# Token groups laid out in fours in the routing of a fused attention, feed-forward and mixture-of-experts kernel

## The chip, the cores and the metric

The kernel runs on one core of a Trainium2 chip. The metric is device time in microseconds (us), from the start to the end of one execution. Several executions were timed, and one more was recorded by the profiler.

A core has a matrix engine (TensorE; PE in the profile, PEld for its weight loads), three engines for elementwise work (VectorE is DVE, ScalarE is ACT, GpSimd is POOL), and queues that start DMA transfers (SP above all). Each engine works through its own list of instructions in order and waits on semaphores for the others.

## The reference, cut to what matters

```python
x = attn(r, k, v, w, u)                  # 4 x 768 tokens, 8 heads of 48: 3072 x 384
h = np.maximum(x @ w_in, 0.0)            # d_ff 2048
x = (h * h) @ w_out
logits = x @ w_gate                      # 3072 x 8
for idx in np.argsort(-logits.flatten()):        # greedy, best pair first
    tok, e = int(idx) // 8, int(idx) % 8
    if assigned[tok] >= 0 or counts[e] >= 384:   # an expert takes 384 tokens
        continue
    assigned[tok] = e; counts[e] += 1
for e in range(8):
    out[assigned == e] = np.maximum(x[assigned == e] @ w1[e], 0.0) @ w2[e]
```

The order of the greedy assignment is what the routing part of the kernel reproduces. Each expert ends with exactly 384 tokens.

## The kernel before, in words

Everything is in float32, and products are formed with each operand split in a high and a low part, so that one product is three matmuls. The program has three stages. Up to about 150 us, the attention is begun together with the preparation of the feed-forward weights. Up to about 591 us, eight blocks of 384 tokens go through the feed-forward layer (`mm1`, line 414, and `mm2`, line 458), with the rest of the attention woven in; in the first part of that a guard (lines 209 to 218) reads the weights once more and takes a minimum on VectorE. From about 601 us, the eight experts are computed one after another (`up`, line 828, and `down`, line 842).

The experts are filled one by one, in the order in which they run full ("phases"). For one phase the 3072 tokens lie as 128 partitions by 24 groups (NG = 24). Each token has its best remaining logit, scaled to a number `yb`. The kernel finds the threshold above which some expert has 384 tokens, in three rounds of a search with 128 steps (NS = 3):

- `above` (line 701) writes, on VectorE, an indicator for each token and each of 128 thresholds: one if `yb` is at least the threshold. It lies in two tiles `I` of 128 thresholds by 12 groups in bfloat16 (GH = 12), made by one instruction each (line 705). The thresholds come from the table `num` (line 531), where each number 0 to 127 stands 24 times; of each 24 the instruction reads the first 12.
- `count` (line 709) sums over tokens on TensorE: 24 weight loads of 128 thresholds, one for each group, each followed by a matmul with the 8 one-hot columns of that group (line 712). For one group the 128 thresholds lie 12 elements, 24 bytes, apart.
- `reached` (line 717) sums a flag over partitions (line 719, the weights are the constant `ones`, which lie side by side), and `narrowed` (line 724) sets the next `yb` and calls `above` again.

After three rounds `choose` (736) and `place` (752) fix the expert and each token's slot. `indices_d` (line 625) writes a one-hot `oi` of the slot for each token, 128 by 24 groups in bfloat16, one VectorE instruction of 3072 elements (line 632). `tokens` (line 639) takes `oi` as weights of 24 matmuls with 6 columns (line 642); there, the 128 weights of one group lie 24 elements, 48 bytes, apart. `gather` (line 650) then fetches the token rows by indirect DMA, and `turn` (line 657) transposes them for the expert.

There are 21 counts (7 phases of 3; the last phase takes what is left) and 8 `tokens`. All of this is put, by lists of numbered slots (FIRST, NEXT, PLAN1, PLAN2, PLAN), between the matmuls of the feed-forward layer's last block and of the experts that run meanwhile. These stages are recorded in the order in which they are written. The stage with the guard, from about 137 to 560 us, is ordered by a scheduler that uses its own estimate of each instruction's duration. The scaled values for the first phase are made there in two pieces: 21 groups early, and 3 groups once the last block's logits are there. The scratch tiles `sm` hold all small tensors of a phase, one behind the other, in words of 4 bytes (class `Small`, line 603); on them the address of `yb` and `ib` depends.

Of the kernel before, what the change touches and what calls it, by code (L numbers as in the profile page):

```python
# [9 lines left out]
BF = mybir.dt.bfloat16  # L10
# [3 lines left out]
OP = mybir.AluOpType  # L14
# [7 lines left out]
def kernel(ctx, tc, r, k, v, w, u, w_in, w_out, w_gate, w1, w2, out):  # L22
    nc = tc.nc
# [11 lines left out]
    E = w_gate.shape[1]  # L35
# [4 lines left out]
    NG = NB * CB  # L40
    NJ = 64
    NT = 128
    GH = NG // 2
# [3 lines left out]
    CT = CAP // 128  # L47
    consts = ctx.enter_context(tc.tile_pool(name="consts", bufs=1))
# [6 lines left out]
                            base=0, channel_multiplier=1)  # L55
# [6 lines left out]
    wk = ctx.enter_context(tc.tile_pool(name="wk", bufs=2))  # L62
# [10 lines left out]
    def piece(shape, dtype, name):  # L73
        return wk.tile(shape, dtype, name=name, tag="w", bufs=NW)
# [45 lines left out]
    g, gk = gt[:, 0], gt[:, 1]  # L120
# [399 lines left out]
    def some():  # L520
        nonlocal pos, todo
        todo += per
        while todo >= 1 and pos < len(segs):
            for x in segs[pos]:
# [3 lines left out]

    LAG = 2

    num = consts.tile([128, 128, NG], BF, name="num")
    nc.gpsimd.iota(num, pattern=[[1, 128], [0, NG]], base=0, channel_multiplier=0,
                   allow_small_or_imprecise_dtypes=True)
    code = consts.tile([128, E], FT, name="code")
    nc.gpsimd.iota(code, pattern=[[-1, E]], base=E, channel_multiplier=0, allow_small_or_imprecise_dtypes=True)
# [11 lines left out]
                            channel_multiplier=-1)  # L547
# [74 lines left out]
    def rp(name="pr"):  # L622
        return abank([128, 512], name)

    def indices_d(st, si):
        sm = st["sm"]
        nc.vector.tensor_scalar(si[:, 1], si[:, 0], 127, None, op0=OP.bitwise_and)
        nc.vector.tensor_scalar(si[:, 2], si[:, 0], 7, None, op0=OP.arith_shift_right)
        ib = sm([128, NG], BF)
        nc.vector.tensor_copy(ib, si[:, 1])  # L630
        st["oi"] = oi = piece([128, 128, NG], BF, "oi")
        nc.vector.tensor_tensor(oi, ib[:, None, :].to_broadcast([128, 128, NG]), num, op=OP.is_equal)
        oq = sm([128, NG, CT], FT)
        nc.vector.tensor_tensor(oq, si[:, 2, :, None].to_broadcast([128, NG, CT]), q3, op=OP.is_equal)
        st["ov"] = ov = sm([128, NG, 2, CT], BF)
        nc.vector.tensor_scalar(ov[:, :, 0], oq, pc, None, op0=OP.mult)
        nc.vector.tensor_tensor(ov[:, :, 1], oq, gg, op=OP.mult)

    def tokens(ph, st):
        p = rp()  # L640
        for g in range(NG):
            nc.tensor.matmul(p[:, :2 * CT], st["oi"][:, :, g], st["ov"][:, g].rearrange("p a b -> p (a b)"),  # L642
                             start=(g == 0), stop=(g == NG - 1))
        f = st["sm"]([128, CT], FT)
        nc.vector.tensor_copy(f, p[:, CT:2 * CT])
        idx = idxs[:, E if ph == "again" else ph]
        nc.vector.scalar_tensor_tensor(idx, f, 128.0, p[:, :CT], op0=OP.mult, op1=OP.add)
        IDX[ph] = idx
# [19 lines left out]
    def route(ph):  # L668
        st = {}

        def best(g0=0, g1=NG):
            n = g1 - g0
            if not g0:
                st["sm"] = sm = Small(2)
                st["v"] = sm([128, NG], FT)
                st["c"] = sm([128, NG, E], FT)
                st["oh"] = sm([128, NG, E], BF)
                st["cc"] = sm([128, NG], FT)
                for nm, shape, dt in (("y", [128, NG], FT), ("yb", [128, NG], BF), ("fl", [128, E], BF),
                                      ("mx", [128, 1], FT)):  # L680
                    st[nm, 0], st[nm, 1] = sm(shape, dt), sm(shape, dt)
                st["y"], st["yb"] = st["y", 0], st["yb", 0]
                halves()
            v, c, oh, cc, y, yb = (st[x][:, g0:g1] for x in ("v", "c", "oh", "cc", "y", "yb"))
            l = lg[:, g0:g1]
            vb = v[:, :, None].to_broadcast([128, n, E])
            nc.vector.tensor_reduce(v, l, axis=X, op=OP.max)
            nc.vector.tensor_scalar(yb, v, rng[:, 3:4], rng[:, 2:3], op0=OP.subtract, op1=OP.mult)
            nc.vector.tensor_tensor(oh, l, vb, op=OP.is_equal)
            above(g0, g1)  # L690
            nc.vector.tensor_tensor(c, l, vb, op=OP.is_equal)
            nc.vector.tensor_tensor(c, c, code[:, None, :].to_broadcast([128, n, E]), op=OP.mult)
            nc.vector.tensor_reduce(cc, c, axis=X, op=OP.max)
            nc.vector.tensor_scalar(y, v, rng[:, 3:4], rng[:, 2:3], op0=OP.subtract, op1=OP.mult)
            nc.vector.tensor_scalar(y, y, 1.0 + SLACK, None, op0=OP.add)


        def halves():
            st["I"] = [wk.tile([128, NT, GH], BF, name="I", tag="dd", bufs=2) for _ in range(2)]

        def above(g0=0, g1=NG):
            for i, t in enumerate(st["I"]):
                a, b = max(g0, i * GH), min(g1, (i + 1) * GH)
                if a < b:
                    nc.vector.tensor_tensor(t[:, :, a - i * GH:b - i * GH],  # L705
                                            st["yb"][:, None, a:b].to_broadcast([128, NT, b - a]),
                                            num[:, :, :b - a], op=OP.is_ge)

        def count(k):
            p = rp()  # L710
            for g in range(NG):
                nc.tensor.matmul(p[:, :E], st["I"][g // GH][:, :, g % GH], st["oh"][:, g], start=(g == 0),  # L712
                                 stop=(g == NG - 1))
            st["fl"] = fl = st["fl", k % 2]
            nc.vector.tensor_scalar(fl, p[:, :E], float(CAP), None, op0=OP.is_ge)
# [8 lines left out]
        def narrowed(k):  # L724
            _, mx = reached(k)
            y = st["y", (k + 1) % 2]
            st["yb"] = yb = st["yb", (k + 1) % 2]
            nc.vector.tensor_scalar(yb, st["y"], mx, float(RAD), op0=OP.subtract, op1=OP.mult)  # L728
            halves()
            above()  # L730
            if k < NS - 2:
                nc.vector.tensor_scalar(y, st["y"], mx, float(RAD), op0=OP.subtract, op1=OP.mult)
                nc.vector.tensor_scalar(y, y, 1.0 + SLACK, None, op0=OP.add)
                st["y"] = y
# [53 lines left out]
        for k in range(0 if steps else NS):  # L788
            steps.append(lambda k=k: count(k))
            steps.append((lambda k=k: narrowed(k)) if k < NS - 1 else lambda: (choose(), fetch(ph)))  # L790
        steps += [place, lambda: indices_d(st, st["si"]), lambda: tokens(ph, st), lambda: gather(ph, st)]
        return best, steps + [lambda q=q: turn(ph, st, q) for q in range(CT)]

# [65 lines left out]
    for g in range(NF, NB * NF):  # L859
        m, f = divmod(g, NF)  # L860
# [37 lines left out]
    for n in range(NF * CB):  # L898
        f, t = divmod(n, CB)
        if f >= NF - LF:  # L900
            t, f = divmod(n - (NF - LF) * CB, LF)
# [8 lines left out]
    for c in range(1, E):  # L910
        s0 = NFE * (c - 2)
        p, first = PLAN1 if c == 1 else PLAN2 if c == 2 else PLAN
# [112 lines left out]
    def exact(ph):  # L1025
# [76 lines left out]
        nc.vector.tensor_copy(si[:, 0], sl)  # L1102
        st = {"sm": sm}
        indices_d(st, si)
        tokens(ph, st)
        gather(ph, st)
        m = sm([128, NG, E], I32)
# [95 lines left out]
```

## Time and profile before

| What | Value |
|---|---|
| runs | 873.54, 874.99, 875.88 us (median 874.99) |
| the profiled execution's own time | 871.84 us |
| its span, first to last instruction | 869.3 us |
| busy share | PE 95%, PEld 90%, DVE 62%, ACT 40%, POOL 16% |
| mean granted TensorE clock | 0.982 of full speed |
| chain that ended last | PE 77%, DMA 6%, DVE 6%, issue 5%, SPq 3%, ACT 2%, POOL 1% |

The chain is followed back from the last instruction to what released each step, so its shares say where the time was spent that could not be hidden. A busy share is an average over stages that differ: VectorE is at 62% over the whole, but at over 80% in the stage of the experts' routing. The profiled execution ran 2.5 us outside its span.

### The profile page before, as it was taken

The numbers are of one execution on the slowest core, as the hardware profiler recorded it, in microseconds if no ns is written. First come the engines' busy times: TensorE is split into PE (matmuls) and PEld (weight loads), VectorE is DVE, ScalarE is ACT, GpSimd is POOL, SyncE is SP. The second block draws the span as 40 slices with busy tenths as digits, with TensorE's granted clock in tenths as the row PEclk, the third lists the DMA queues.
The fourth block names the chain that finished last, engine by engine and source line by source line (L and its number), as shares of the span: only waits on it lengthen the run. The fifth ranks groups of instructions, "written<-read, shape, count | busy, mean of one in ns | idle before, by whom it ended". The sixth has DMA issues, their size and how long they took to land.

```text
span 869.3 us, 15596 instructions
## 1 busy us (share of the span) xinstructions
PE 822.3 (95%) x6069; PEld 779.2 (90%) x6069; DVE 540.5 (62%) x1172; ACT 349.1 (40%) x761; POOL 136.3 (16%) x188
## 2 busy tenths in 40 slices
PE   5669999999999999999999999997989999999996
PEld 4569988899999999999999999896989999999996
DVE  6969879864445444444435435646977888885551
ACT  4467554335325334435335324302333443334441
POOL 5402103111111111111111000001102113113311
PEclk9989999999999999999999999997999999999999
DMA  9998357842122122122121000013334355345430
GB/s 178 186 222 201 84 143 216 238 104 56 28 41 55 29 41 55 29 42 55 28 38 33 1 15 27 1 43 121 115 97 128 119 155 161 104 137 164 146 119 31
DMA packets 120211, 82.32 MB, mean 95 GB/s; under 512 B 80321, under 2 KB 111681, under 8 KB 120129
## 3 DMA queue, kind: packets, MB, share of 16 engines
q1 hardware_dynamic: 114608, 69.14, 31.8%
q0 software_dynamic: 3072, 9.44, 3.4%
q10 hardware_dynamic: 2448, 2.66, 1.5%
q8 instruction: 50, 0.82, 0.4%
q14 instruction: 33, 0.26, 0.1%
HBM read 69.42 MB, written 9.44 MB: 91 GB/s over the span
## 4 chain that ended last, share of the span: by engine, by line
PE 77%; DMA 6%; DVE 6%; issue 5%; SPq 3%; ACT 2%; POOL 1%; POOLq 0%; DVEq 0%
PE acc L458 21%; PE p L414 21%; PE q L828 10%; PE ad L842 9%; PE pr L712 3%; DMA raw<-in_moe_w_in_dram 3%; PE pa L331 2%; PE py L345 2%; PE py L351 2%; PE pr L642 2%; DMA gd<-in_moe_w_out_dram 1%; DVE lg L218 1%; SPq L87 1%; PE pu L384 1%; PE lt L475 1%
## 5 line engine op out<-in xcount | busy, mean ns | idle before, releaser
L414 PE MATMUL p<-xT,wi 128*128 128x384 f32 x1152 | 227.2, 342 | 10.6 <-DMA xT<-xT 7.0
L414 PEld LDWEIGHTS p<-xT,wi 128*128 128x128 f32 x1152 | 205.0, 190 | 14.2 <-issue 7.4
L458 PE MATMUL acc<-wo,h 128*128 128x392 f32 x1008 | 204.2, 347 | 0.0
L458 PEld LDWEIGHTS acc<-wo,h 128*128 128x128 f32 x1008 | 177.4, 188 | 4.9 <-issue 2.6
L425 DVE TENSOR_TENSOR s<-a,p 128x384 f32<-128x384 f32 x112 | 61.8, 553 | 144.7 <-ACT a L420 144.6
L420 ACT ACTIVATE a<-p 128x384 f32<-128x384 f32 x128 | 62.3, 488 | 164.9 <-PE p L414 131.8
L842 PE MATMUL ad<-we,he 128*128 128x384 f32 x576 | 117.8, 345 | 0.0
L828 PE MATMUL q<-xe,we 128*128 128x384 f32 x576 | 114.8, 343 | 0.8 <-ACT xe L665 0.6
L828 PEld LDWEIGHTS q<-xe,we 128*128 128x128 f32 x576 | 102.4, 191 | 1.8 <-ACT xe L665 0.8
L842 PEld LDWEIGHTS ad<-we,he 128*128 128x128 f32 x576 | 100.8, 191 | 0.4 <-issue 0.4
L831 ACT ACTIVATE he<-q 128x384 fp32r<-128x384 f32 x64 | 31.5, 493 | 143.7 <-PE q L828 123.0
L432 ACT ACTIVATE h<-s 128x384 fp32r<-128x384 f32 x112 | 58.8, 526 | 70.5 <-DVE s L425 64.1
L437 DVE TENSOR_TENSOR h<-s,h 128x384 fp32r<-128x384 f32 x112 | 63.3, 567 | 20.1 <-ACT h L432 19.7
L295 ACT ACTIVATE dd<-ident,c 128x128 f32<-128x128 f32 x192 | 59.1, 392 | 18.2 <-DVE c L289 10.5
L832 DVE SCALAR_TENSOR_TENSOR he<-q,he 128x384 fp32r<-128x384 f32 x64 | 35.6, 556 | 46.9 <-ACT he L831 46.6
L83 POOL MEMSET rkv<- 128x384 f32 x24 | 9.8, 418 | 261.4 <-PE py L345 261.4
L849 POOL DMA_INDIRECT out_dram<-oe,idxs x24 | 27.7, 1155 | 140.2 <-ACT oe L847 136.8
L336 DVE COPY_PREDICATED dd<-msk,pa 128x512 f32<-128x512 int32 x48 | 33.9, 734 | 21.1 <-PE pa L331 21.1
L654 POOL DMA_INDIRECT xg<-x,idxs x24 | 25.9, 1080 | 103.5 <-DVE sm L728 33.0
L705 DVE TENSOR_TENSOR I<-sm,num 128x1536 bf16<-128x1536 bf16 (+2 forms) x43 | 39.1, 948 | 0.5
L712 PEld LDWEIGHTS <-I 128*128 128x128 bf16 x504 | 31.9, 159 | 6.2 <-DVE I L705 3.0
L283 POOL TENSOR_TENSOR tmp<-rkv 128x384 f32<-128x384 f32 x24 | 27.3, 1139 | 54.4 <-ACT s L423 31.8
(192 smaller groups left out, 987.3 us busy)
## 6 DMA issues: line engine op xcount, KB each, us to landing
w1r<-in_moe_w_dram SPq DMA_DIRECT2D x32, 384.0 KB, 3.1
w2r<-in_moe_w_dram SPq DMA_DIRECT2D x32, 384.0 KB, 3.8
raw<-in_moe_w_out_dram SPq DMA_DIRECT2D x8, 768.0 KB, 5.4
gd<-in_moe_w_in_dram SPq DMA_DIRECT2D x16, 384.0 KB, 3.6
gd<-in_moe_w_out_dram SPq DMA_DIRECT2D x16, 384.0 KB, 3.9
rkv<-in_k_dram SPq DMA_DIRECT2D x24, 192.0 KB, 3.2
rkv<-in_r_dram SPq DMA_DIRECT2D x24, 192.0 KB, 4.1
rkv<-in_v_dram SPq DMA_DIRECT2D x24, 192.0 KB, 4.7
```

The costliest lines, as they stand in the source:

```text
L295: nc.scalar.activation(d[:, h], ident, AF.Copy, scale=c[:, h:h + 1])
L414: nc.tensor.matmul(p, WI[f // PO][:, wl, d, fs], x[:, hl, d], start=(n == 0), stop=(n == 3 * KD - 1))
L420: nc.scalar.activation(a, p, AF.Relu)
L425: nc.vector.tensor_tensor(s, a, p, op=OP.mult)
L432: nc.scalar.activation(h[:, 0], s, AF.Copy)
L437: (eng or nc.vector).tensor_tensor(h[:, 1], SM.pop(f), h[:, 0].bitcast(FT), op=OP.subtract)
L458: nc.tensor.matmul(acc[t][:, c0:], h[:, hl, t * 128:(t + 1) * 128], WO[f // PO][:, wl, f % PO, c0:], start=(f == 0 and n == 0), stop=(f == ...
L705: nc.vector.tensor_tensor(t[:, :, a - i * GH:b - i * GH], st["yb"][:, None, a:b].to_broadcast([128, NT, b - a]), num[:, :, :b - a], op=OP. ...
L712: nc.tensor.matmul(p[:, :E], st["I"][g // GH][:, :, g % GH], st["oh"][:, g], start=(g == 0), stop=(g == NG - 1))
L828: nc.tensor.matmul(p, wt[:, wl, d, fs], x[:, hl, d], start=(n == 0), stop=(n == 3 * KD - 1))
L832: nc.vector.scalar_tensor_tensor(h[:, 1], p, 0.0, h[:, 0].bitcast(FT), op0=OP.max, op1=OP.subtract)
L842: nc.tensor.matmul(ac2[t], h[:, hl, t * 128:(t + 1) * 128], wt[:, wl, f % P2], start=(f == 0 and n == 0), stop=(f == NFE - 1 and n == 2))
```

## The change

The table `num` holds each number 4 times instead of 24. The indicators are laid out as (3 fours of groups) x 128 thresholds x 4 groups in each of the two tiles, and the one-hots as 6 x 128 x 4. For one group, the 128 weights of a load now lie 4 elements, 8 bytes, apart. One instruction still makes a whole tile: it runs over fours of groups, within these over the 128 numbers, within these over 4 groups. Where a piece doesn't begin or end on a four, `above` issues an instruction more.

```diff
-    num = consts.tile([128, 128, NG], BF, name="num")
-    nc.gpsimd.iota(num, pattern=[[1, 128], [0, NG]], base=0, channel_multiplier=0,
+    NP_ = 4
+    num = consts.tile([128, 128, NP_], BF, name="num")
+    nc.gpsimd.iota(num, pattern=[[1, 128], [0, NP_]], base=0, channel_multiplier=0,
...
-        st["oi"] = oi = piece([128, 128, NG], BF, "oi")
-        nc.vector.tensor_tensor(oi, ib[:, None, :].to_broadcast([128, 128, NG]), num, op=OP.is_equal)
+        st["oi"] = oi = piece([128, NG // NP_, 128, NP_], BF, "oi")
+        nc.vector.tensor_tensor(oi, ib.rearrange("p (a o b) -> p a o b", o=1, b=NP_).to_broadcast([128, NG // NP_, 128, NP_]),
+                                num[:, None].to_broadcast([128, NG // NP_, 128, NP_]), op=OP.is_equal)
...
-            nc.tensor.matmul(p[:, :2 * CT], st["oi"][:, :, g], st["ov"][:, g].rearrange("p a b -> p (a b)"),
+            nc.tensor.matmul(p[:, :2 * CT], st["oi"][:, g // NP_, :, g % NP_], st["ov"][:, g].rearrange("p a b -> p (a b)"),
...
-            st["I"] = [wk.tile([128, NT, GH], BF, name="I", tag="dd", bufs=2) for _ in range(2)]
+            st["I"] = [wk.tile([128, GH // NP_, NT, NP_], BF, name="I", tag="dd", bufs=2) for _ in range(2)]
...
-                if a < b:
-                    nc.vector.tensor_tensor(t[:, :, a - i * GH:b - i * GH],
-                                            st["yb"][:, None, a:b].to_broadcast([128, NT, b - a]),
-                                            num[:, :, :b - a], op=OP.is_ge)
+                while a < b:
+                    o = a % NP_
+                    n = NP_ if not o and b - a >= NP_ else min(NP_ - o, b - a)
+                    m = (b - a) // NP_ if n == NP_ else 1
+                    x = (a - i * GH) // NP_
+                    nc.vector.tensor_tensor(
+                        t[:, x:x + m, :, o:o + n],
+                        st["yb"][:, a:a + m * n].rearrange("p (a o b) -> p a o b", o=1, b=n).to_broadcast([128, m, NT, n]),
+                        num[:, None, :, :n].to_broadcast([128, m, NT, n]), op=OP.is_ge)
+                    a += m * n
...
-                nc.tensor.matmul(p[:, :E], st["I"][g // GH][:, :, g % GH], st["oh"][:, g], start=(g == 0),
+                nc.tensor.matmul(p[:, :E], st["I"][g // GH][:, g % GH // NP_, :, g % NP_], st["oh"][:, g], start=(g == 0),
```

TensorE, ScalarE and the SP queue have the same instructions in the same order as before. VectorE and GpSimd differ at three places. The first is VectorE where the first phase's indicators for 21 groups are made (`keep` and `s` belong to the feed-forward layer's last block, `rng` to the scaling). Before:

```order
L437 TENSOR_TENSOR keep<-s,keep 128x384
L705 TENSOR_TENSOR I<-sm,num 128x1536
L425 TENSOR_TENSOR s<-a,p_5709 128x384
L705 TENSOR_TENSOR I<-sm,num 128x128x9
L437 TENSOR_TENSOR keep<-s,keep 128x384
```

And of the changed kernel:

```order
L437 TENSOR_TENSOR keep<-s,keep 128x384
L711 TENSOR_TENSOR I<-sm,num 128x1536
L425 TENSOR_TENSOR s<-a,p_5709 128x384
L711 TENSOR_TENSOR I<-sm,num 128x1024
L711 TENSOR_TENSOR I<-sm,num 128x128
L437 TENSOR_TENSOR keep<-s,keep 128x384
```

The second tile's 9 groups are made by two instructions, 8 groups and 1 group. The second place is VectorE at about 144 us, in the guard (`gd` is a piece of weights, `lg` here its running minimum, `c`, `rkv` and `dd` belong to attention unit 6, `s` and `h` to the feed-forward layer). Before:

```order
L425 TENSOR_TENSOR s<-a,p_1574 128x384
L218 SCALAR_TENSOR_TENSOR lg_66<-gd,lg_66 128x192
L277 TENSOR_TENSOR rkv<-rkv,tk 128x8x48
L437 TENSOR_TENSOR h_1588<-s,h_1588 128x384
L289 TENSOR_REDUCE c<-tmp 128x8
L218 SCALAR_TENSOR_TENSOR lg_66<-gd,lg_66 128x192
L336 COPY_PREDICATED dd<-msk,pa 128x4x128 x2
L425 TENSOR_TENSOR s<-a,p_1623 128x384
```

And of the changed kernel:

```order
L425 TENSOR_TENSOR s<-a,p_1574 128x384
L277 TENSOR_TENSOR rkv<-rkv,tk 128x8x48
L289 TENSOR_REDUCE c<-tmp 128x8
L437 TENSOR_TENSOR h_1588<-s,h_1588 128x384
L218 SCALAR_TENSOR_TENSOR lg_66<-gd,lg_66 128x192 x2
L336 COPY_PREDICATED dd<-msk,pa 128x4x128
L425 TENSOR_TENSOR s<-a,p_1623 128x384
L336 COPY_PREDICATED dd<-msk,pa 128x4x128
```

The scheduler counts the shorter table as done earlier, and lets two attention steps go ahead of pieces of the guard; some ten rows later the two orders agree again. The third place is GpSimd just before, where the tables are made: one memset (`rkv`, line 83) now stands behind three short instructions for `tri`, `ones` and `onef` instead of ahead of them.

## Rows read from the trace of the kernel before

**Rows 1.** The page's chain that ended last, by line.

```profile
PE acc L458 21%; PE p L414 21%; PE q L828 10%; PE ad L842 9%; PE pr L712 3%; DMA raw<-in_moe_w_in_dram 3%; PE pa L331 2%; PE py L345 2%; PE py L351 2%; PE pr L642 2%; DMA gd<-in_moe_w_out_dram 1%; DVE lg L218 1%; SPq L87 1%; PE pu L384 1%; 
```

**Rows 2.** Windows: stretch, its us, then busy us by engine, clock, DMA.

```profile
600.00:633.00 33.00, 30.14 (x219) 27.46 (x220) 27.23 (x68) 11.84 (x20) 4.10 (x6) 0.86 0.45 131
633.00:666.00 33.00, 30.14 (x213) 28.78 (x212) 24.90 (x69) 10.79 (x20) 8.01 (x9) 0.95 0.33 103
...
732.00:765.00 33.00, 33.00 (x256) 31.80 (x255) 27.49 (x68) 12.58 (x24) 7.14 (x9) 1.00 0.43 133
```

**Rows 3.** Chain of waits in order of time, 720 to 746 us: start, us, what.

```profile
722.88 1.65 PE pr L642 x24
...
733.12 1.45 PE pr L712 x24
...
740.53 1.41 PE pr L712 x24
```

**Rows 4.** Groups by line and shape: count | busy us, mean ns | idle before.

```profile
L705 DVE TENSOR_TENSOR I<-sm,num 128x1536 bf16<-128x1536 bf16 x41 | 37.5, 954 | 0.5
...
L632 DVE TENSOR_TENSOR oi<-sm,num 128x3072 bf16<-128x3072 bf16 x8 | 14.1, 1759 | 0.3
...
L705 DVE TENSOR_TENSOR I<-sm,num 128x1152 bf16<-128x1152 bf16 x1 | 0.9, 902 | 0.0
...
L705 DVE TENSOR_TENSOR I<-sm,num 128x384 bf16<-128x384 bf16 x1 | 0.7, 743 | 0.0
```

**Rows 5.** The same view, weight loads whose weights lie strided, and side by side.

```profile
L712 PEld LDWEIGHTS <-I 128*128 128x128 bf16 x504 | 31.9, 159 | 6.2 <-DVE I L705 3.0 <-issue 2.1 <-DVE sm L695 0.5
...
L642 PEld LDWEIGHTS <-oi 128*128 128x128 bf16 x192 | 13.9, 176 | 1.3 <-issue 1.3
...
L719 PEld LDWEIGHTS <-ones 128*128 128x128 bf16 x21 | 2.1, 101 | 2.1 <-issue 1.8
```

**Rows 6.** Timeline, 745.2 to 745.5 us: two pairs with weights side by side.

```profile
745.16 0.10 PEld L755 LDWEIGHTS <-ones 128*128 128x128 bf16 x1 [0.16 <-issue]
745.17 0.19 PE L755 MATMUL pr<-sm,ones 128*128 128x24 bf16 x1
745.18 0.10 PEld L756 LDWEIGHTS <-tri 128*128 128x128 bf16 x1
745.21 0.17 PE L756 MATMUL pr<-sm,tri 128*128 128x24 bf16 x1
```

**Rows 7.** Waits of PE, 545 to 860 us: total us, times, longest.

```profile
PE pr L593 <- DVE m L591: 2.9, 1, 2.9
PE px L663 <- DMA xg<-x,idxs: 2.3, 3, 1.4
PE pr L712 <- DVE I L705: 1.8, 2, 1.5
```

**Rows 8.** Chain of waits, 590 to 606 us, before the first expert.

```profile
596.93 3.98 DMA xg<-x,idxs
...
600.96 0.92 PE px L663 x3
```

**Rows 9.** Timeline of all engines, 738.6 to 741.9 us: a third round's indicators and count.

```profile
738.70 1.83 DVE L705 TENSOR_TENSOR I<-sm,num 128x1536 bf16<-128x1536 bf16 x2
...
740.37 1.57 PE L712 MATMUL pr<-sm,I 128*128 128x8 bf16 x24
```

**Rows 10.** Timeline of all engines, 624 to 627 us: the second expert's indices and gather.

```profile
625.50 0.15 DVE L645 COPY sm<-pr 128x3 f32<-128x3 f32 x1
...
626.64 0.95 POOL L654 DMA_INDIRECT xg<-x,idxs  x1 [25.30 <-DVE idxs L647]
```

**Rows 11.** Chain of waits, 150 to 172 us, in the guard.

```profile
161.38 4.45 DMA gd<-in_moe_w_out_dram
...
168.57 3.10 PE p L414 x9
```

**Rows 12.** Groups by line: the table's instruction on POOL.

```profile
L532 POOL IOTA num<- 128x3072 bf16 x1 | 3.3, 3341 | 0.0
```

## The prediction

> **What bounds the kernel now.** I read the chain that ended last first. Nearly all of its weight lies on TensorE: the feed-forward layer and the experts, and behind them 3% on line 712 (the counts) and 2% on line 642 (the token sums) [rows 1]. Then the windows. In the routing of the middle phases TensorE is busy for 33.0 of 33 us at the full clock, with VectorE at 27.5; in the first 66 us of the experts TensorE leaves 2.9 us in each 33 and VectorE works 27.2 and 24.9 [rows 2]. So a TensorE instruction saved there comes off the end, as long as VectorE, which has some 5.5 us to spare per phase of 33 us, delivers in time. The chain in order of time gives the price of the two loops that the change touches: 24 pairs of weight load and matmul take 1.41 to 1.45 us in a count and 1.65 us in the token sum [rows 3], that is 60 and 69 ns for one pair. The columns that stream through (8 and 6) can't explain that; the fewer take longer. What differs is how far apart the weights lie: one load takes 159 ns at 24 bytes, 176 ns at 48 bytes, and 101 ns where they lie side by side, 2 bytes apart [rows 5].
>
> **TensorE: 29 loops with weights 8 bytes apart.** No row shows 8 bytes. From one side, it is no better than 24 bytes: 60 ns, and the counts win nothing (the token sums 9 ns a pair). From the other, it is like side by side. The two pairs with such weights that follow each other start their matmuls 40 ns apart (745.17 and 745.21) and their loads 20 ns apart [rows 6]; that is a pair alone, and a stream of 24 might run below 40. A straight line from 40 ns at 2 bytes to 60 at 24 gives 45 at 8. The value lies 6 bytes from the one row and 16 from the other, so I keep near the first and take 42 ns; the ends that I keep are 30 (halfway between the starts of loads and of matmuls) and 60. At 42 a count gets shorter by 24 x 18 ns = 0.43 us and a token sum by 24 x 27 ns = 0.65 us. The 504 loads of line 712 are 21 counts, the 192 of line 642 are 8 token sums [rows 5]. Where they lie decides what arrives:
> - Three counts and one token sum stand between the last matmuls of the feed-forward layer. They end that layer earlier, and with it the stores that the first gather waits for: 3 x 0.43 + 0.65 = 1.94 us.
> - Two counts fall into the wait for that gather (it is 3.98 us, and the first transpose comes at 600.96) [rows 8]: 0.
> - One count at 609 us: 0.43.
> - One token sum and two counts lie at 621 to 632 us, 1.51 us. The second expert's gather starts at 626.64, behind indices that come at 625.50 [rows 10] out of VectorE's queue, which is full there [rows 2], and transposes have waited for gathers already (2.3 us in three waits) [rows 7]. TensorE would only wait longer; I count 0.2.
> - One count at 636 us: 0.43. The wait for line 591 behind it (2.9 us) [rows 7] starts from TensorE's own result, and moves along.
> - One token sum and three counts at 656 to 676 us; the last one's result waits in VectorE's queue, so 0.65 + 2 x 0.43 + 0.2 = 1.71.
> - Five token sums and nine counts from 689 us on, where TensorE has no gap: 5 x 0.65 + 9 x 0.43 = 7.12.
>
> Together 1.94 + 0.43 + 0.2 + 0.43 + 1.71 + 7.12 = 11.8 us. With 30 ns in place of 42 it is 18.5, with 60 ns only the 9 ns of the token sums are left, 7 x 0.22 = 1.5.
>
> The Trainium skill has a rule for this spacing (Advanced Engine Details and Errata, SBUF Cachelines): the memory is read in lines of 16 bytes, and a reader keeps its full speed if it takes at least two elements of each line. At 8 bytes there are two weights to a line, at 24 and 48 one; by it a pair would cost the 40 ns of the side-by-side row, and the sum would be 13.0 us in place of 11.8. The trace agrees as far as it goes (101 ns against 159 and 176).
>
> **VectorE: the same elements in shorter runs.** The whole tiles keep their 1536 and 3072 elements. The rows at 954 and 1759 ns give 0.524 ns for an element and 149 ns fixed [rows 4], so two elements a cycle are being made now, with runs of 12 and 24. For runs of 4 I take no extra cost. The bounds: nothing is gained, since the elements stay. Against me stands the form with runs of 9, which should take 753 ns by that slope and takes 902 [rows 4]: 149 ns for 128 runs, 1.16 ns each. With 384 runs of 4 that would be 0.45 us on each indicator and, with 768, 0.89 us on each one-hot. The end of the scale is that the pairing is lost: 0.80 and 1.61 us. I stay at 0, because the 9 is odd and leaves half a pair in every run, as 4 and 12 do not. If the cover goes, the third count of a phase suffers first. Its second indicator ends at 740.53, 0.16 us after the count has begun at 740.37 [rows 9]; it is needed by the count's second half only, 0.72 us in now and 0.50 us in at 42 ns. So 0.3 us remain.
>
> One page speaks against the one-hots alone: the Trainium skill (Vector Engine (DVE) Microarchitecture Reference, Measured stream behaviour on trn2) has full rate for runs of two words of 4 bytes that start on an 8-byte boundary, and 1.30 against 1.05 ns where they start on the odd word. By the code's scratch layout `yb` starts even and `ib` odd. That is up to 0.4 us on a one-hot as an estimate by that page, off the path except at 617 us; the sum would be 11.4. No run of 4 stands in this trace.
>
> The first phase's early piece is two instructions instead of one of 902 ns: 149 + 1024 x 0.524 = 686 ns, and one of 128 elements between 216 and 743 ns, the latter by the row of 384 in runs of 3 [rows 4]. That is 0 to 0.5 us more while the feed-forward layer leaves VectorE idle between blocks: 0.
>
> **GpSimd and the guard.** The table's instruction takes 3.34 us for 3072 numbers [rows 12]; a sixth of the numbers saves up to 2.8 us on an engine that nothing waits for here: 0. The order that changes with it lies at 144 us, where VectorE waits for the guard's loads (one of 4.45 us) and TensorE behind it resumes only at 168.57 [rows 11]. Two attention steps move ahead of pieces of the guard. A load can slip by a turn either way: between 1.5 us gained and 1.5 us lost, and I take 0.
>
> **The sum.** The profiled execution took 871.84 us, 869.3 of span and 2.5 around it; it lies 3.15 below the median of 874.99. 871.84 - 11.8 = 860.0 for a profiled execution, and 874.99 - 11.8 = 863.2 for the median.
>
> **The rivals.**
> - Half the way: loads at 8 bytes are better than at 24, but each still pays for most of its lines, 50 to 55 ns a pair; with VectorE's queue eating some, 4 to 7 us are left: 869.5. For it: a load grows quickly from 2 to 24 bytes (58 ns) and slowly from there to 48 (17 ns) [rows 5], so much may be lost early.
> - No change: the pair's pace is that of issuing, not of reading, and the spacing only lengthens what lies behind. Then 60 ns stay, and 874 is the time. Against it: the token sum has the same instructions and takes 69 [rows 3], and one pair took 40 [rows 6]. In the Trainium skill, TensorE: Matmul & The Clock Gate (Wait — 56ns, not 53.3ns?) gives about 62 ns for a matmul that the sequencer decodes in software; by that the counts stay at 60 ns. The 40 ns of the trace stand against it.
> - Slower: VectorE becomes the bound. If runs of 4 lose the pairing, a phase of six indicators and one one-hot costs VectorE 6 x 0.80 + 1.61 = 6.4 us more, 33.9 in place of 27.5 [rows 2], over the 33.0 that TensorE took. Each third count then waits over 1 us for its indicators, and the gathers of the first phases come later by as much; 0.9 us for five full phases and some 4 us for the crowded stretch 609 to 646 make 883. It decides from an extra of 5.5 / 8 = 0.7 us per indicator (a one-hot counted as two). The price of the odd runs, 0.45, would stay below and cost about half the gain.
>
> **How the numbers follow.** The forecast has 0.52, half the way 0.24, no change 0.12, slower 0.12. The likeliest is 863.2 us. The range begins at 858, near the 18.5 us of 30 ns a pair, and ends at 874: it takes in half the way and the first half of no change, and leaves out slower. A difference below 0.3% (2.6 us) can't be told from none here. Faster by more takes the first two, and a part of no change in which the token sums and the guard help: 0.79. Within: 0.09. Slower: 0.12.
>
> **What would show it.** In the changed profile, 24 pairs of a count should take about 1.0 us in the chain and a token sum the same, with loads at 100 to 120 ns; the indicators stay at 954 ns and the one-hots between 1.76 and 2.2 us. The first transpose should come 1.9 us earlier, and the stretch from 699 to 765 us should be shorter by 3.9 us for two phases. If loads stay at 159 ns, the step on spacing is wrong; if the indicators exceed 1.4 us, the one on short runs; if both hold and the end doesn't move, TensorE's waits for VectorE have grown.

## The result, and the profile after

The changed kernel takes 859.57 us (median of 4 runs, 857.46 to 861.95) where the one before takes 874.26 (median of 4 runs: the three of the table above and one of 872.85): ratio 0.9836, with a 95% interval from 0.9815 to 0.9857, or 12.5 to 16.2 us less. Its profiled execution took 861.02 us with a span of 858.6, so it is 10.8 us shorter than the profiled one of before. The forecast was 863.2, 11.8 us less.

The chain that ended last, by line, has lost most of the two loops, line 712 and 642 of [rows 1] (now 720 and 644). VectorE's share of it went from 6% to 10%, and a weight split of the experts (line 823) stands in it now:

```profile
PE acc L458 21%; PE p L414 21%; PE q L836 8%; PE ad L850 7%; PE pa L331 2%; PE py L345 2%; PE py L351 2%; DMA gd<-in_moe_w_out_dram 2%; DMA raw<-in_moe_w_in_dram 2%; DVE we L823 2%; SPq L87 1%; DVE I L711 1%; PE pr L720 1%; PE pu L384 1%; P
```

A count and a token sum now take the same time in the chain, where they took 1.41 to 1.45 and 1.65 us [rows 3]:

```profile
651.09 0.80 PE pr L644 x24
...
655.14 0.81 PE pr L720 x24
```

That is 33 ns for a pair in both. The groups by line and shape answer to [rows 4, 5]:

```profile
L711 DVE TENSOR_TENSOR I<-sm,num 128x1536 bf16<-128x1536 bf16 x41 | 37.5, 954 | 0.5
...
L720 PEld LDWEIGHTS <-I 128*128 128x128 bf16 x504 | 18.7, 118 | 7.1 <-DVE I L711 4.1 <-issue 2.4 <-DVE sm L694 0.6
L633 DVE TENSOR_TENSOR oi<-sm,num 128x3072 bf16<-128x3072 bf16 x8 | 14.1, 1759 | 0.3
...
L644 PEld LDWEIGHTS <-oi 128*128 128x128 bf16 x192 | 7.0, 118 | 1.3 <-issue 1.3
...
L711 DVE TENSOR_TENSOR I<-sm,num 128x1024 bf16<-128x1024 bf16 x1 | 0.7, 685 | 0.0
L711 DVE TENSOR_TENSOR I<-sm,num 128x384 bf16<-128x384 bf16 x1 | 0.5, 455 | 0.0
L711 DVE TENSOR_TENSOR I<-sm,num 128x128 bf16<-128x128 bf16 x1 | 0.4, 441 | 0.0
```

A load fell from 159 and 176 ns to 118. VectorE pays nothing at all for runs of four: 954 and 1759 ns, to the nanosecond. PE's waits from 545 to 850 us (total, times, longest) have another first row:

```profile
PE pr L727 <- DVE sm L723: 7.1, 8, 1.5
PE pr L594 <- DVE m L592: 2.9, 1, 2.9
PE px L665 <- DMA xg<-x,idxs: 2.5, 3, 1.7
PE pr L720 <- DVE I L711: 2.4, 4, 1.5
```

`sm` of line 723 is the flag that VectorE makes of a count, and line 727 sums it over partitions. Before, the same wait was short (lines 715 and 719; [rows 7] leaves this row out):

```profile
PE pr L719 <- DVE sm L715: 1.2, 3, 0.6
```

The timeline of VectorE around the first count of a phase shows why TensorE waits for the flag. Before, in the fourth expert, VectorE and then TensorE:

```profile
726.94 0.95 DVE L815 TENSOR_TENSOR we<-w1r,we 128x768 fp32r<-128x768 f32 x1
...
728.07 0.55 DVE L832 SCALAR_TENSOR_TENSOR he<-q,he 128x384 fp32r<-128x384 f32 x1
728.73 0.17 DVE L715 TENSOR_SCALAR sm<-pr 128x8 bf16<-128x8 f32 x1
```

```profile
727.12 1.57 PE L712 MATMUL pr<-sm,I 128*128 128x8 bf16 x24
...
729.17 0.18 PE L719 MATMUL pr<-sm,ones 128*128 128x8 bf16 x1
```

And after the change, at the same place:

```profile
717.93 1.82 DVE L711 TENSOR_TENSOR I<-sm,num 128x1536 bf16<-128x1536 bf16 x2
...
721.13 0.95 DVE L823 TENSOR_TENSOR we<-w1r,we 128x768 fp32r<-128x768 f32 x1
...
722.26 0.55 DVE L840 SCALAR_TENSOR_TENSOR he<-q,he 128x384 fp32r<-128x384 f32 x1
722.73 0.16 DVE L723 TENSOR_SCALAR sm<-pr 128x8 bf16<-128x8 f32 x1
```

```profile
720.47 0.97 PE L720 MATMUL pr<-sm,I 128*128 128x8 bf16 x24
...
722.94 0.17 PE L727 MATMUL pr<-sm,ones 128*128 128x8 bf16 x1 [0.88 <-DVE sm L723]
```

The count now ends at about 721.4. The flag starts at 722.73, because a weight split of the expert (line 823), the indices and a product of the expert stand ahead of it in VectorE's queue. Before, the same three stood there too, but count and token sum were so long that VectorE was through (728.62) as the count ended, and the flag started at once.

### The profile page after: what moved, and what is told of

Read it like the earlier page. It is cut to its first block, busy times and chain, and to the rows that moved or that the text cites. A ratio compares the mean times of both kernels' runs of the same rounds, so it can differ in the third digit from the quotient of the medians.

```text
span 858.6 us, 15596 instructions
## 1 busy us (share of the span) xinstructions
PE 806.1 (94%) x6069; PEld 761.8 (89%) x6069; DVE 535.9 (62%) x1173; ACT 348.0 (41%) x761; POOL 132.9 (15%) x188
## 4 chain that ended last, share of the span: by engine, by line
PE 71%; DVE 10%; issue 5%; DMA 5%; SPq 3%; ACT 2%; POOL 2%; ACTq 0%; POOLq 0%; DVEq 0%
PE acc L458 21%; PE p L414 21%; PE q L836 8%; PE ad L850 7%; PE pa L331 2%; PE py L345 2%; PE py L351 2%; DMA gd<-in_moe_w_out_dram 2%; DMA raw<-in_moe_w_in_dram 2%; DVE we L823 2%; SPq L87 1%; DVE I L711 1%; PE pr L720 1%; PE pu L384 1%; PE lt L475 1%
## 5 line engine op out<-in xcount | busy, mean ns | idle before, releaser
L857 POOL DMA_INDIRECT out_dram<-oe,idxs x24 | 27.2, 1132 | 135.0 <-ACT oe L855 131.5
L656 POOL DMA_INDIRECT xg<-x,idxs x24 | 24.6, 1024 | 100.9 <-PE pr L727 31.5
L711 DVE TENSOR_TENSOR I<-sm,num 128x1536 bf16<-128x1536 bf16 (+3 forms) x44 | 39.0, 925 | 0.5
L823 DVE TENSOR_TENSOR we<-w1r,we 128x768 fp32r<-128x768 f32 x32 | 30.5, 954 | 2.3 <-ACT we L822 2.3
```

The source lines that it names most:

```text
L711: nc.vector.tensor_tensor(t[:, x:x + m, :, o:o + n], st["yb"][:, a:a + m * n].rearrange("p (a o b) -> p a o b", o=1, b=n).to_broadcast([12 ...
L823: nc.vector.tensor_tensor(t[:, 1], d["raw"][j], t[:, 0].bitcast(FT), op=OP.subtract)
```

## The experiments

Each ratio is against the kernel before, run beside it on the same chip. The runs were made in three groups, on three chips, where the kernel before took 874.51, 872.86 and 874.37 us (medians), so kernels of different groups are best compared by their ratios. An expert's period is the time from its first matmul of `up` to that of the next expert; from the third expert on, the full phases, with a token sum and three counts, lie in the third, fourth and fifth expert's periods, and the sixth's and seventh's have a token sum and no counts. The texts of what was expected call the fourth and fifth period the fifth and sixth.

**Counts alone.** Only `I` is in fours, read from the table of before (edit against the changed kernel, two of its places).

```diff
-    num = consts.tile([128, 128, NP_], BF, name="num")
+    num = consts.tile([128, 128, NG], BF, name="num")
...
-        st["oi"] = oi = piece([128, NG // NP_, 128, NP_], BF, "oi")
+        st["oi"] = oi = piece([128, 128, NG], BF, "oi")
...
```

> Only the indicators of the counts lie in fours; the one-hots of the token sums stay 48 bytes apart, and the table keeps 24 of each number (the indicators read the first 4, so with gaps). Theory spacing: a pair in a count at 34 ns, a pair in a token sum at 69 ns, indicators at 954 ns. Each count is 0.62 us shorter; the token sums no longer bring the first count of a phase forward, so that TensorE's wait for the flag behind it shrinks from about 1.0 us to about 0.2 us, and a full phase wins 1.6 to 1.7 us as in the changed kernel. Time 9 to 10 us below before. Rival, that the gaps in the table are what counts: indicators slower than 954 ns or counts at 60 ns, and little of the gain.

Measured: 866.92 us, ratio 0.9908 (0.9879 to 0.9937), about 8.0 us less, where 9 to 10 were expected; the counts fell to 0.80 us, the token sums stayed, and the wait for the flag is 3.0 us in all, against 7.1 with the whole change. In its profile the fourth and fifth expert's periods are 31.35 and 31.31 us, the same as with the whole change (33.03 and 32.99 before). In a full phase the token sum's gain is thus lost entirely in the wait for the flag; behind the third expert it arrives only where there are no counts (27.2 us for 28.06 in the sixth and seventh period).

**Token sums alone.** Only `oi` is in fours (edit against the kernel before).

```diff
-        st["oi"] = oi = piece([128, 128, NG], BF, "oi")
-        nc.vector.tensor_tensor(oi, ib[:, None, :].to_broadcast([128, 128, NG]), num, op=OP.is_equal)
+        st["oi"] = oi = piece([128, NG // NP_, 128, NP_], BF, "oi")
+        nc.vector.tensor_tensor(oi, ib.rearrange("p (a o b) -> p a o b", o=1, b=NP_).to_broadcast([128, NG // NP_, 128, NP_]),
+                                num[:, None, :, :NP_].to_broadcast([128, NG // NP_, 128, NP_]), op=OP.is_equal)
...
```

> Only the one-hots of the token sums lie in fours (read from the table with gaps); the indicators are as before. Theory spacing: a pair in a token sum at 34 ns, so 0.85 us less for each of the eight, a pair in a count stays at 60 ns. In a full phase about half is lost, since the first count then comes before VectorE is through with the flag's queue: 0.4 to 0.5 us of 0.85. In all 4 to 5 us below before. If VectorE's queue does not matter, 6 to 7 us.

Measured: 870.11 us, ratio 0.9941 (0.9920 to 0.9962), 5.2 us less. A full phase of 33.0 us takes 32.6, so 0.4 of 0.85 us arrive, as expected (the wait for the flag is 2.5 us in all, for 1.2 before); phases without counts get the whole of it (27.2 for 28.1).

**The whole change with the long table.** The layouts of the change, read from a table with 24 of each number.

```diff
-    num = consts.tile([128, 128, NP_], BF, name="num")
-    nc.gpsimd.iota(num, pattern=[[1, 128], [0, NP_]], base=0, channel_multiplier=0,
+    num = consts.tile([128, 128, NG], BF, name="num")
+    nc.gpsimd.iota(num, pattern=[[1, 128], [0, NG]], base=0, channel_multiplier=0,
...
```

> The whole change, but the table keeps 24 of each number, 4 of which are read: gaps of 40 bytes, the long instruction on GpSimd, and the guard in the order of before. Theory spacing: pairs at 34 ns, indicators at 954 ns and one-hots at 1759 ns as in the changed kernel, and the time only 1.1 us above it (the second block of the feed-forward layer begins 1.1 us earlier in the changed kernel's profile than before; that should go). So about 13 us below before. Rival, the gaps count for VectorE: indicators above 1.0 us, TensorE waits for them, and half of the gain or more is gone.

Measured: 863.24 us, ratio 0.9867 (0.9835 to 0.9899), 11.6 us less, where 13 were expected. Pairs, indicators and one-hots are those of the changed kernel. Gaps in the table cost VectorE nothing; whether the shorter table, and the order in the guard that goes with it, win the last two or three us can't be told, since the intervals overlap.

**Other spacings.** Two kernels with other group sizes, each layout with its own table without gaps.

```diff
-    NP_ = 4
+    NP_ = 6            # in the second kernel 2
+    NO_ = 8            # for oi; in the second kernel 3
...
```

> Other spacings: indicators in sixes (weights of a count 12 bytes apart), one-hots in eights (weights of a token sum 16 bytes apart), each with its own table without gaps. If what counts is how many weights lie in one stretch of 16 bytes, then 16 bytes apart (one each) costs as much as 24: about 60 ns a pair; 12 bytes apart (three of four stretches hit, a third of them twice) lies between 34 and 60, about 45 to 50 ns. If the pace grows in a straight line from 34 ns at 8 bytes to 60 at 24: 41 ns at 12 and 47 ns at 16 bytes. VectorE as in the changed kernel (954 and 1759 ns). Time between the changed kernel and before, about 8 us below before.

> Closer spacings: indicators in twos (4 bytes apart), one-hots in threes (6 bytes apart), tables without gaps. TensorE: if 34 ns is the floor of a pair, both stay at 34 ns; if the read still counts at 8 bytes, they fall below, towards 30. VectorE: runs of two are one word of 4 bytes and runs of three are odd; if short runs cost VectorE anything, it shows here: indicators at 1.2 to 1.6 us instead of 954 ns, one-hots above 2.2 us instead of 1759 ns, and with 1.6 us VectorE is over-full and the time 10 us or more above the changed kernel. If runs are free whatever their length, the time is that of the changed kernel.

Measured: 866.89 us (0.9918, 0.9887 to 0.9949) and 862.04 us (0.9868, 0.9834 to 0.9901). The chain of waits of the first (12 bytes in line 724, 16 in line 648):

```profile
721.35 1.47 PE pr L648 x24
725.54 1.12 PE pr L724 x24
```

and of the second (4 bytes in line 724, 6 in line 648):

```profile
766.21 0.60 PE pr L724 x24
781.00 0.63 PE pr L648 x24
```

and the second's groups by line and shape:

```profile
L715 DVE TENSOR_TENSOR I<-sm,num 128x1536 bf16<-128x1536 bf16 x41 | 37.5, 954 | 0.5
L637 DVE TENSOR_TENSOR oi<-sm,numo 128x3072 bf16<-128x3072 bf16 x8 | 18.3, 2292 | 0.3
L724 PEld LDWEIGHTS <-I 128*128 128x128 bf16 x504 | 14.6, 98 | 7.9 <-DVE I L715 5.0 <-issue 2.7
```

The first kernel's indicators of 3 groups leave a gap in the output behind each run of three, which is taken up below:

```profile
L715 DVE TENSOR_TENSOR I<-sm,num 128x384 bf16<-128x384 bf16 x2 | 1.2, 597 | 0.0
```

With [rows 3] and the lines after the change this gives a pair's pace for seven spacings. (A count's matmul has 8 columns and a token sum's 6; at 8 bytes both take 33 ns, so the two can stand in one table.)

| bytes between weights | 4 | 6 | 8 | 12 | 16 | 24 | 48 |
|---|---|---|---|---|---|---|---|
| 24 pairs, us | 0.60 | 0.63 | 0.80 | 1.12 | 1.47 | 1.43 | 1.65 |
| one pair, ns | 25 | 26 | 33 | 47 | 61 | 60 | 69 |
| stretches of 16 bytes hit by 128 weights | 32 | 48 | 64 | 96 | 128 | 128 | 128 |

From 8 to 16 bytes the pace grows by 14 ns for each 32 stretches, at 24 bytes it is where it was at 16, and 6 bytes lie on the same line (26); at 4 bytes, where the line would give about 20, it is 25, the least that these runs show. A straight line in bytes, the first kernel's other theory, would have put 16 bytes at 47 ns and is excluded. What makes 48 bytes slower again stays open. In the second kernel the shorter loops brought no time, with one-hots that take longer (below) and 9.6 us of waiting for the flag, for 7.1 in the changed kernel.

On VectorE, runs of two are free as well, and runs of three cost 533 ns over 1024 runs, 0.52 ns each, where the output is written without gaps: a run costs when it is odd, not when it is short. The 9 of [rows 4] (1.16 ns each) is not only odd but leaves a gap in the output, and the gap costs too. The same 128 runs of three take 455 ns with their starts 8 bytes apart (lines after the change), 597 with 12 (the line above) and 743 with 24 ([rows 4]). Even runs with a gap in the output stand in no run.

**Moved splits, first try.** The changed kernel with four weight splits placed behind the flag.

```diff
-REST = [1, 2, 6, 16, 18]
+REST = [1, 2, 6, 20, 22]
...
-PLAN2 = (..., [60, 62, 66, 72, 74, 78, 86, 87])
+PLAN2 = (..., [62, 62, 66, 72, 74, 83, 86, 87])
-PLAN = (..., [52, 54, 63, 63, 65, 74, 78, 85])
+PLAN = (..., [52, 54, 63, 63, 65, 74, 83, 85])
```

> The changed kernel with four weight splits of the experts moved some quarter slots later, behind the flag of the first count (78 to 83 in two of the lists, 60 to 62, and 16 and 18 to 20 and 22). Theory: what the changed kernel lost, about 1.0 us in each phase, it lost to TensorE's wait for the flag (7.1 us in 8 waits), which stands behind a split of 0.95 us in VectorE's queue. With the split behind it the wait falls to under 0.3 us a phase, the half clock after the wait at 689 us goes, and the time falls 4 to 7 us below the changed kernel, about 19 us below before. Rival, VectorE is the bound as a whole (28.9 us of 32): the wait turns up elsewhere, at the second count or at the products, and less than 2 us are won.

Measured: 862.77 us, ratio 0.9860 (0.9829 to 0.9890), no better than the changed kernel. The expectation failed, but not everywhere: the fourth and fifth expert's periods were 30.50 and 30.48 us for 31.35 and 31.31, as forecast, while in the early phases TensorE waited for the very splits that had been moved back (4.1 us in three waits, one of 2.6), and the wait for the flag remained at 3.7.

**One split moved, and two more moved ahead.** First only the change to `PLAN` above; then with it, in `PLAN2`, two splits earlier, where VectorE was idle.

```diff
-PLAN2 = (..., [60, 62, 66, 72, 74, 78, 86, 87])
+PLAN2 = (..., [58, 62, 66, 72, 74, 75, 86, 87])
```

> The changed kernel with one split moved behind the first flag in the list of the later phases alone (78 to 83), since that gave 0.85 us for each full phase there, and the other moves cost it again before the experts' products. Expected: the two periods that begin with the fifth and sixth expert at 30.5 us instead of 31.35, the others as in the changed kernel, so 1.7 to 2.5 us below the changed kernel, 16 to 17 us below before. Rival, VectorE is the bound as a whole: no gain.

> As the kernel with one split moved, and in the third expert's list two splits are moved to earlier places instead of later ones (60 to 58, 78 to 75), where VectorE had idle time. Expected: the waits at 669 us (1.1 us) and 688 us (1.2 us, with the half clock after it, 1.7 us) go as well: 4 to 6 us below the changed kernel. Rival: the weights to be split have not landed or their buffers are not free that early, then VectorE's queue is held and nothing is won.

Measured: 860.29 us (0.9834, 0.9807 to 0.9862) with one, 854.74 us (0.9784, 0.9757 to 0.9812) with three. The second is some 5 us below the changed kernel by the ratios, with intervals that just meet. In the kernel with three, the queue around the first count has the flag 0.9 us earlier after the start of the indicators, 3.93 us behind it for 4.80, with the split gone from between:

```profile
717.65 1.82 DVE L711 TENSOR_TENSOR I<-sm,num 128x1536 bf16<-128x1536 bf16 x2
...
721.11 0.55 DVE L840 SCALAR_TENSOR_TENSOR he<-q,he 128x384 fp32r<-128x384 f32 x1
721.58 0.16 DVE L723 TENSOR_SCALAR sm<-pr 128x8 bf16<-128x8 f32 x1
```

The third expert's period is 31.25 us where the changed kernel's two profiles (the second one stands further down) have 33.49 and 32.06, the fourth's and fifth's 30.45 for 31.35 and 30.46 for 31.31. From 677 us on TensorE waits 0.2 us for the flag, for 2.8 in the changed kernel. One move alone gave its 0.85 us for each of two phases in the profile, but its time can't be told from the changed kernel's.

**The same moves without the change.** The kernel before with the three moved splits.

> The kernel before with the three moved splits (78 to 83 in the later phases, 60 to 58 and 78 to 75 in the third expert's list), and nothing else. Theory: before, the first flag's place in VectorE's queue cost TensorE nothing (the count was long enough), so the moves alone win under 2 us of the 874. Rival, the moved splits help by themselves, whatever the layout: 4 us or more below before, and then part of what the moved kernel won isn't the layout's loss given back.

Measured: 874.92 us, ratio 1.0004 (0.9982 to 1.0026). In its profile the third, fourth and fifth period are 33.06, 33.06 and 32.99 us, for 33.06, 33.03 and 32.99 before. The moves win nothing by themselves. What they win after the change is part of what the change had lost to the flag.

**The changed kernel again.**

> The changed kernel once more, on the chip and beside the runs that the moved ones are compared with: 13 to 16 us below before, as in its first runs.

Measured: 860.84 us, ratio 0.9841 (0.9808 to 0.9874). Its profiled execution had a span of 853.0 us, 5.6 less than the first one of the same program. The windows tell where (stretch, us, busy by engine, granted clock, DMA). First profile:

```profile
168.00:171.00 3.00, 3.00 (x14) 2.56 (x14) 2.48 (x7) 2.66 (x9) 0.00 (x0) 0.50 1.00 377
642.00:645.00 3.00, 3.00 (x13) 3.00 (x12) 1.52 (x5) 1.14 (x3) 0.35 (x1) 0.56 0.17 65
690.00:693.00 3.00, 3.00 (x12) 3.00 (x11) 2.39 (x5) 0.00 (x0) 2.39 (x3) 0.53 0.73 206
```

second profile:

```profile
168.00:171.00 3.00, 3.00 (x29) 2.88 (x25) 2.29 (x8) 2.38 (x8) 0.00 (x0) 1.00 0.88 311
642.00:645.00 3.00, 3.00 (x19) 3.00 (x18) 2.79 (x6) 1.89 (x5) 2.57 (x5) 1.00 0.18 68
690.00:693.00 3.00, 2.67 (x30) 2.33 (x28) 3.00 (x5) 1.75 (x4) 0.00 (x0) 1.00 0.69 205
```

In the first execution TensorE ran at 1.2 GHz at these three places (0.50 to 0.56, where a stretch takes in the rise), in the second at 2.4 (1.00). The same times do not hold quite the same work in both, but the second profile's granted clock is 1.00 in all of 60 to 590 us and of 604 to 845 us, so the half clock is not just elsewhere. Ahead of the first place TensorE waited 2.4 us in the first profile and 1.0 in the second. Ahead of the other two the waits were alike in both, 2.9 us for line 592 and 1.0 us for the flag, so the same wait can be followed by the half clock or not. The periods of the second and third expert, in which these two places lie, are 36.94 and 33.49 us in the first profile and 35.34 and 32.06 in the second: the flag's wait cost 1.4 us more than itself in one execution.

**Twos, with the moved splits.** The last step that the runs point to (edit against the kernel with three moved splits).

```diff
-    NP_ = 4
+    NP_ = 2
```

> Both layouts in twos (4 bytes apart) and the three moved splits. A pair at 26 ns in all 29 loops, indicators at 954 ns; the one-hots in runs of two, so not odd, at 1759 ns if only odd runs cost VectorE anything (2292 in threes). Against fours with the same moves a count and a token sum are 0.19 us shorter each, 5.5 us in all, of which VectorE's queue takes about half: 2 to 3 us below the kernel in fours with moved splits, 20 to 22 us below before. Rival: VectorE is full, the wait for the flag grows by what the loops get shorter, and the time is the same.

Measured: 853.07 us, ratio 0.9757 (0.9729 to 0.9785): 21.2 us below before, the fastest of all. Pairs took 26 ns, indicators 954 and one-hots 1758 ns. Against fours with the same moves it is 1.7 us by the medians and 2.4 by the ratios, with intervals that overlap: a full phase takes 30.42 us for 30.46, since the wait for the flag takes what the loops give (6.5 us in nine waits again), and 27.03 for 27.25 where there are no counts.

## Why the prediction was right, and where it was not

- *TensorE bounds, and these loops lie on its chain*: right. Each layout alone gave a gain (8.0 and 5.2 us), and with both it is 14.3 by the ratio.
- *42 ns a pair*: mis-sized. It is 33 ns, near the end of 30 that was kept for the range. A count lost 0.62 us instead of 0.43, a token sum 0.85 instead of 0.65. By the prediction's own places, with these two savings in its sum, this would have been 2.7 + 0.6 + 0.2 + 0.6 + 2.3 + 9.8 = 16.2 us. The step that failed was to put 8 bytes close to the 40 ns of the pair that stood alone: that pair is not the floor, a stream reaches 25 ns at 4 bytes.
- *From 689 us on, TensorE has no gap, so all of it arrives*: wrong. Of the 9.8 us, the span from the third expert's start to the end gave 4.5 us in one profile (187.4 us for 191.8) and 6.2 in the other (185.6). The prediction looked for the cover at the third count's indicators; from 677 us on TensorE waits for none of these, before or after, and it was the first count's flag that VectorE delivered late (2.8 us in three waits). VectorE's 5.5 us to spare per phase did not help, since what counts is what stands ahead of the flag in its queue. With the splits moved the same span is 183.3 us: 8.5 of the 9.8 arrive.
- *Up to the gather 1.94 us, two counts behind it nothing*: the last matmul of the feed-forward layer starts at 589.2 instead of 593.2 us, 4.0 earlier, of which 1.2 were there before the layer's last block began and 2.7 arose in it, in the loops (2.7 is what 33 ns a pair give). The two counts in the gather's wait won nothing, as forecast: the first expert starts 4.0 us earlier too.
- *The sum*: close in part by luck. It was 4.4 us too low by the loops and 3.6 to 5.3 too high behind the third expert's start, and these two nearly cancelled. By parts (up to the first expert's start, from there to the third's, behind it) the forecast was 1.9, 2.8 and 7.1 us; the profiles have 4.0, 2.2 and 4.5, and 6.2, 3.9 and 6.2. What the second one has more comes with the guard and with the clock.
- *The guard, 0 with 1.5 us either way*: the second block of the feed-forward layer's first product (line 414) lasts 74.5 us from start to start before, 73.0 and 70.8 in the two profiles of the changed kernel. But other kernels with the old order show 73.4 to 74.6 and with the new one 72.4 to 75.9, so no effect of the order is shown, and the swing is wider than the bound.
- *VectorE, nothing for runs of four*: right, with the reason given (odd runs cost, short ones do not), which the threes and twos confirm; the runs of 9 in [rows 4], from which it was argued, also paid for the gap behind them. The 0.4 us for one-hots that start on an odd word, an estimate by a page of the Trainium skill (Vector Engine (DVE) Microarchitecture Reference, Measured stream behaviour on trn2), does not appear: 1759 ns, unchanged.
- *Two weights in 16 bytes give full speed* (the Trainium skill, Advanced Engine Details and Errata, SBUF Cachelines): half right. From 6 to 24 bytes the pace goes with the stretches of 16 bytes that are touched, but two weights in each (8 bytes apart) still cost 33 ns where four (4 bytes) cost 25.
- *Half the way, no change, slower*: none came. The first would need 50 ns a pair; 47 is what 12 bytes give.

## What to carry to other kernels

From 6 to 24 bytes between the 128 weights of a load, a pair's pace went with the number of 16-byte stretches they touch (26 to 61 ns). So lay out a bfloat16 operand that VectorE writes for many small matmuls in groups that keep them close, if its runs stay even and leave no gap. When a loop on the bounding engine gets shorter, look for what it used to cover: read from the queue of the other engine what stands ahead of the next thing that the loop's follower waits for, and move it. Test such a move on the old kernel too, to see whether it is the change's loss that comes back.

## What the runs showed of the hardware that was not expected

A weight load and its small matmul can follow each other every 25 ns (24 pairs in 0.60 us at 4 bytes). VectorE's 954 ns for 1536 bfloat16 results hold when one input is read again in runs of two, as in runs of twelve. And the same program's profiled span differed by 5.6 us between two executions (858.6 and 853.0), with the half clock present at three places in one and at none of them in the other.
